# A transformer block with MLP on one core: deadline-ordered loads, DMA transposes for the first y tiles, two equal rounds of chunk widths, warming matmuls, a new item order and a new clock model

## The chip, the cores and the metric

One core of a Trainium2 chip. The time is the device time of one execution in microseconds (us). Most executions of one kernel agree within 0.3%, so this study uses five rounds a kernel, each beside runs of the kernel before on the same chip. A ratio is the mean time of one kernel's fast runs over that of the kernel before in the same rounds, so it is not quite the ratio of the medians beside it. PE is the matmul engine (TensorE) and PEld its weight loads, ACT is ScalarE, DVE is VectorE, and SPq is the queue of SyncE that issues the DMAs.

## The reference

```python
x  = A_x                                   # 2048 tokens x 1024, bf16
xn = layernorm(x)
s  = attention(xn, A_wqkv, A_wo)           # 32 heads of 32
y  = layernorm(xn)                         # a second normalisation
g  = silu(gelu(y @ B_w1 + B_b1) @ B_w2 + B_b2)   # 1024 -> 3584 -> 1024
return x + s * g
```

## The kernel before

The program is built from 512 *attention units*, four heads at a time. A unit has score matmuls on PE, two exponentials on ACT (128x1024 each), and value and sum matmuls on PE. All other matmul work is cut into *items* that fill PE between a unit's scores and the values of the unit before: `a` (first MLP matmul, one block of 128 features for one token chunk), `w` (second MLP), `q` and `v` (queries and keys, values, of the next heads), `o` (output projection). The string `PLAN` says which item goes with which unit, from unit 7 on; units 0 to 6 belong to the prologue, which normalises and transposes x. `w3` is one item cut over three units, and `.` is a unit without filler. In the views, `war` holds MLP weights, `wq` those of the projections, `hT` the first MLP's result and `gT` the second's; buffers are reused, so a name can also stand for other data.

```python
chunks = []                                # token chunks of q, a and w items
while t0 < S:                              # 352 x 5, then 288
    chunks.append((t0, min(CW, S - t0))); t0 += CW

def clock(self, x, eng, dma, c, rdy):      # estimated times, used only to order work
    ...
    elif eng == "tensor":
        mode, rounds, n = c
        one = n / 2.4 + 2.5
        span = rounds * one
        if mode != self.pe_mode:
            t = max(t, self.clk[eng] + 103.0)
            span += max(120.0 - one, 0.0)

def fill_act(u):                           # a tanh goes ahead of unit u's exponentials if it seems to fit
    ...
        if t + cost - rdy <= ATOL or u - u0 >= AGE: act_tasks.pop(0); fn()

# prologue, unit p
if p >= 2: ynorm_pro(p - 2)                # y of tiles 0 to 2 on ACT, then stored to HBM
if 4 <= p: load_sub(0, p - 4)              # first MLP weights
pair_kq(p); ...; pair_v(p)                 # 3 PSUM banks in rotation: pro_banks = [4, 5, 7]
...
if u == 5:                                 # y of the first chunk read back, transposed, from HBM
    for s4 in range(4): load_y(0, s4)
```

The clock estimate never runs on the chip. It decides, while the program is generated, in which order VectorE and ACT get their instructions. Cuts are marked with dots.

The softmax here doesn't subtract the row's maximum and nothing guards it: scores larger than these inputs give would overflow.

Of the kernel before, what the change touches and what calls it, by code (L numbers as in the profile page):

```python
# [13 lines left out]
q a v a a a . a q a v a v a a a q a a v a q a a v q a a v a a q a q a a v q a q a a a q q v a a q w3 w4 w3 w4 v w4 w2 w2 w2 a a v a q v v a q q a a a a a q a q a a q a a v a q a q q a a a v v a a a q v a a a a q q a a w3 v w3 w4 w4 w4 q v q v w2 v q w3 w3 a a a v v q a a a q a a q q a a a q q a v a q a v a a q a q a a a a v a a q a q v v v a a q q q v a q q a w3 q v q w5 q w4 w3 q w3 w4 w2 w4 a a a v v a a q a a q a q q v a a q a q v a q a a a a q a a a q a a v a a a a v a v a q a v q q w3 w4 v q w4 w4 w4 v w4 w3 w4 a a a q q a a a a v a v a a a a a v q a a v a a a q a a a v a a q q v a q q a a q a q q q a v w3 v w4 w4 q w4 w4 w4 w4 w4 a a a a q q a a q a a q a a a q a q q a a a a a a a a a a q q a a a a a q a q w2 w4 w3 w4 w2 w3 w5 o o o o o o o o o o o o w4 o o o o o o o o o o o o o o o o o o o o o o o o o o o . o o o o o o o . o o  # L14
# [21 lines left out]
class _Prog:  # L36
# [24 lines left out]
    def clock(self, x, eng, dma, c, rdy):  # L61
        t = max(self.clk[eng], rdy)
        if dma:
            self.clk[eng] = t + 60.0
            self.dma_clk = max(t, self.dma_clk) + 4.4 * c
            x.t = self.dma_clk + 1700.0
        elif eng == "tensor":
            mode, rounds, n = c
            one = n / 2.4 + 2.5
            span = rounds * one  # L70
            if mode != self.pe_mode:
                t = max(t, self.clk[eng] + 103.0)
                span += max(120.0 - one, 0.0)
            self.pe_mode = mode
            self.clk[eng] = t + span
            x.t = t + span + 140.0
        elif eng == "scalar":
            t = max(self.clk[eng], rdy + 40.0)
            self.clk[eng] = t + c
            x.t = t + c + 115.0  # L80
        elif eng == "vector":
            self.clk[eng] = t + c - 85.0
            x.t = t + c
        else:
            self.clk[eng] = t + c
            x.t = t + c
# [81 lines left out]
def bass_recurrent_scan__mha_block__mixer_channel_mlp__prompt_kernel(  # L168
# [23 lines left out]
    LAG = 1  # L192
# [7 lines left out]
    chunks = []  # L200
    t0 = 0
    while t0 < S:
        chunks.append((t0, min(CW, S - t0)))
        t0 += CW
# [6 lines left out]
    with ExitStack() as st:  # L211
# [68 lines left out]
        wq_due = []  # L280
        wq_of = {}

        def load_wq(hp, which=(0, 1, 2), lo=0, hi=DC):
            for t3 in which:
                src = A_wqkv[:, t3 * D + hp * 256:t3 * D + (hp + 1) * 256].rearrange("(c p) n -> p c n", p=128)
                op("sync", lambda e, src=src, t3=t3: e.dma_start(wq[:, t3, lo:hi, :], src[:, lo:hi, :]),  # L286
                   w=[("wq", t3, s) for s in range(lo // 2, hi // 2)], dma=f"wq{t3}{lo}", c=64 * (hi - lo))
                for s in range(lo // 2, hi // 2):
                    wq_of[t3, s] = hp

        def wq_part():
            hp, t3, lo = wq_due.pop(0)
            load_wq(hp, (t3,), lo, lo + 2)

        def wq_ready(hp, t3, dc):
            while wq_of[t3, dc // 2] != hp:
                wq_part()
# [7 lines left out]
        for tb in range(4, NT):  # L305
            load_x(tb)
        op("gpsimd", lambda e: e.iota(iota_i, pattern=[[1, 128]], base=0, channel_multiplier=-1), w=["iota"])
# [3 lines left out]

        def load_bias():
            op("sync", lambda e: e.dma_start(brow[0:FB, :], B_b1.rearrange("(fb p) -> fb p", p=128)), w=["b1r"], dma="b1", c=8)
            op("sync", lambda e: e.dma_start(brow[FB:FB + DC, :], B_b2.rearrange("(nb p) -> nb p", p=128)), w=["b2r"], dma="b2", c=8)
# [57 lines left out]
        TDMA = 4  # L372
# [6 lines left out]
        def transp(tb):  # L379
            i = tb % NXN  # L380
            if tb >= TDMA:
                op("sync", lambda e: e.dma_start_transpose(xnT[:, :, tb * 128:(tb + 1) * 128], xnb[i]),
                   r=[("xnb", i)], w=[("xnT", tb)], dma=f"xt{tb % 4}", c=256)
                return
            bk = pro_bank()

            def f(e):
                for dc in range(DC):
                    ins = e.transpose(bankb(bk)[:, dc * 128:(dc + 1) * 128], xnb[i][:, dc * 128:(dc + 1) * 128], ident[:])
                return ins  # L390
            op("tensor", f, r=[("xnb", i), "ident"], w=[("b", bk)], c=("full", 8, 128))
            op("scalar", lambda e: e.activation(xnT[:, :, tb * 128:(tb + 1) * 128],
                                                bankb(bk)[:, 0:D].rearrange("p (c t) -> p c t", c=DC), ACT.Copy),
               r=[("b", bk)], w=[("xnT", tb)], c=903.0)
# [87 lines left out]
        sp_tasks = defaultdict(list)  # L482

        def load_sub(g, q):
# [8 lines left out]
            op("sync", lambda e: e.dma_start(dst[:, lo:hi, :], src[:, lo:hi, :]), w=[("war", s, q)], dma=f"war{s}{q}", c=256)  # L493

        def load_piece(g):

            if g >= NPC:
                return
            k = g % 11
            if k < 7:  # L500
                subs = [0, 1, 2, 3]
            elif k == 7:
                subs = [0, 1, 2, 3]
            else:
                subs = [0, 1, 2, 3, 4, 5, 6]
            for i, q in enumerate(subs):
                sp_tasks[cur["u"] + i].append((load_sub, g, q))
            if k == 4:
                for i, q in enumerate((4, 5, 6)):
                    sp_tasks[cur["u"] + 1 + i].append((load_sub, g + 3, q))  # L510

        def load_y(c, s):
            t0, n = chunks[c]
            op("sync", lambda e: e.dma_start_transpose(yTc[:, 2 * s:2 * s + 2, 0:n], y_d[t0:t0 + n, 256 * s:256 * s + 256]),
               r=[("y", t) for t in toks(t0, n)], w=[("yTc", s)], dma=f"yTc{s}", c=200)

        def w1_item(c, f):
# [8 lines left out]
            def step(dc, bk):  # L526
                op("tensor", lambda e: mm4(e, lambda j: bankq(bk, j, 0, n),
                                           lambda j: w1v[s][:, dc, fo + 32 * j:fo + 32 * j + 32],
                                           yTc[:, dc, 0:n], dc == 0, dc == DC - 1),
                   r=[("war", s, dc // 2), ("yTc", dc // 2)], w=[("b", bk)], c=("col", 1, n))  # L530

            def fin(bk):
# [36 lines left out]
                if f == FB - 1 and c + 1 < NCH:  # L569
                    for s4 in range(4):  # L570
                        sp_tasks[cur["u"] + 2 + 2 * s4].append((load_y, c + 1, s4))
            return Item([lambda bk, dc=dc: step(dc, bk) for dc in range(DC)], fin, pre=pre)

        def w2_item(c, nb):
# [8 lines left out]
            def step(f, bk):  # L583
                hurry(lambda: (c, f) in have)
# [30 lines left out]
        def load_wo(h):  # L615
            op("sync", lambda e: e.dma_start(wo_sb[:, h, :], A_wo[h * 128:(h + 1) * 128, :]), w=[("wo", h)], dma=f"wo{h % 4}", c=256,
               after=[tail["xfree"]])

        def load_xres(tb):
            i4 = tb % NTB  # L620
            op("sync", lambda e: e.dma_start(xres[i4], x2[tb * 128:(tb + 1) * 128, :]), w=[("xres", i4)], dma=f"rx{i4}", c=256,
               after=[tail["xfree"]])

        def load_gres(tb):
# [5 lines left out]
               r=[("gT", nb, c) for nb in range(DC) for c in cs], w=[("gres", i4)], dma=f"rg{i4}", c=500, after=[tail["xfree"]])  # L630

        def wo_item(tb, k):
# [3 lines left out]
            def pre():  # L636
                if k == 0:
                    assert ("wo", HG - 1) in pg.lastw
                    if tb == 0:
                        for t in range(NTB):  # L640
                            load_gres(t)
                    elif tb + NTB - 1 < NT:
                        load_xres(tb + NTB - 1)
                        load_gres(tb + NTB - 1)

            def step(hc, bk):
                hurry(lambda: (hc, tb // 2) in scaled)
# [5 lines left out]
            def fin(bk):  # L653
                m = cnt["wo"]
                cnt["wo"] += 1
                f2, o3 = m % 2, tb % 3
                run_dq(pg.ready("vector", r=[("b", bk), ("gres", i4)]) + TOL)
# [68 lines left out]

        for p in range(3):
# [4 lines left out]
        def pro_unit(p):  # L732
            if p + 3 < NP:
                norm_pair(p + 3)
            if p == 3:
                load_bias()
            if p >= 2:
                ynorm_pro(p - 2)
            if 4 <= p:
# [9 lines left out]
        def ynorm_pro(tb):  # L749
            if tb < 3:  # L750
# [3 lines left out]
                op("sync", lambda e: e.dma_start(y_d[tb * 128:(tb + 1) * 128, :], xt), r=[("xst", tb)], w=[("y", tb)], dma=f"yst{tb % 4}", c=256)  # L754
# [149 lines left out]
        while u < NU + LAG or state["qi"] < total or dq or act_tasks:  # L904
# [3 lines left out]
            if u == 5:  # L908
                for s4 in range(4):
                    load_y(0, s4)  # L910
# [10 lines left out]
            if u >= NP - 1 and state["qi"] < total:  # L921
# [3 lines left out]
                for hp, which in loads.pop(qi, ()):  # L925
                    if hp < HG // 2:
                        wq_due.extend((hp, t3, lo) for t3 in reversed(which) for lo in range(0, DC, 2))
                if wq_due:
                    for _ in range(4 if qi == 0 else 1):
                        wq_part()  # L930
# [7 lines left out]
                for v in sorted(k for k in sp_tasks if k <= u):  # L938
                    for fn, *a in sp_tasks.pop(v):
                        fn(*a)  # L940
                if entry:
                    for s in it.steps[lo:hi]:
                        s(state["bank"])
                    if ys and (len(dq) < 3 or u >= 32):
                        ynorm(ys.pop(0))
                    if hi == len(it.steps):
                        it.finish(state["bank"])
                if state["qi"] == q_end:
                    tail["xfree"] = pg.lists["tensor"][-1]
                    for h in range(HG):  # L950
                        sp_tasks[u + 1 + 2 * h].append((load_wo, h))
                    for t in range(NTB):
                        sp_tasks[u + 2 + 4 * t].append((load_xres, t))
# [58 lines left out]
```

## Time and profile before

| | before |
|---|---|
| median of three runs | 1102.12 us |
| profiled span | 1098.9 us |
| PE / ACT / VectorE busy | 98% / 95% / 57% |
| unit 7 starts | 49.6 us |
| units 7 to 511 | 1031.3 us |
| after the start of unit 511 | 17.9 us |

The first lines are from the page of the kernel before: busy time of each engine, and the chain of work that ended last, by engine and by line.

```profile
...
PE 1074.6 (98%) x29089; PEld 700.4 (64%) x29089; DVE 629.1 (57%) x1413; ACT 1041.3 (95%) x1190; POOL 20.0 (2%) x63
...
q8 instruction: 228, 3.74, 1.4%
...
PE 57%; ACT 40%; DVE 1%; DMA 1%; issue 0%; SPq 0%; POOL 0%
ACT P L836 36%; PE ps L398 34%; PE ps L824 9%; PE ps L853 6%; PE ps L856 6%; ACT u L558 3%; PE ps L675 1%; PE ps L691 1%; DVE stats L326 1%; DMA OT<-in_A_x_dram 1%; ACT thz L601 0%; DMA wq<-in_A_wqkv_dram 0%; DMA xnT<-hT 0%; DVE hT L359 0%;
...
```

PE and ACT both look full and share the chain. The Trainium skill, page "Perfetto Trace Analysis", section "Identifying the Most-Contended Engine", warns that "matmul busy % (`TensorMatrix` occupancy) is not a good measure of how close you are to roofline". So I use another measure throughout. The score matmuls of each unit have their own line, and their first start in the timeline is the start of the unit. For a unit with a filler of r rounds of width n, undisturbed units of the trace fit

*floor = 0.887 us + r (n/2400 + 0.0012) us*,

that is 2.07 us for an 8-round, 352-wide item (median measured 2.073). The *excess* of a unit is its measured length less this floor, and the excess of units 7 to 511 is what PE lost: **18.5 us** before. The floor summed over all these units, 1012.8 us, is the same for both kernels. ACT needs two exponentials of 0.903 us (start to start) and about 0.68 us for each tanh, which serves two `a` items.

The timeline of PE in the prologue of the kernel before (start, duration, engine, line, operation, tile, count, and idle time ahead with what ended it):

```profile
...
7.54 1.89 PE L389 MATMUL ps<-ident,hT 128*128 128x128 bf16 x16 [7.54 <-DVE hT L359]
10.70 3.57 PE L675 MATMUL ps<-xnT,wq 128*128 128x256 bf16 x16 [1.27 <-ACT xnT L392]
...
17.44 1.92 PE L675 MATMUL ps<-xnT,wq 128*128 128x256 bf16 x16
...
21.04 0.40 PE L824 MATMUL ps<-QT,KT 32*128 32x256 bf16 x8
...
23.52 1.70 PE L675 MATMUL ps<-xnT,wq 128*128 128x256 bf16 x14 [1.53 <-DMA xnT<-hT]
```

L389 is the transposes of two tiles, L675 a query/key group, L824 the scores that begin a unit (17.11 and 21.04 us for units 0 and 1). The first group takes 3.57 us, later ones 1.92: about half the speed. At 23.52 PE waits for the DMA transpose of tiles 4 and 5.

The issuing queue (SPq) around the first filler units, and PE's waits from 49 to 66 us (total, times, longest), of the kernel before:

```profile
...
45.04 5.17 SPq L514 DMA_TRANSPOSE yTc<-y_scratch  x4
50.25 1.09 SPq L493 DMA_DIRECT2D war<-in_B_w_dram  x2
```

```profile
...
PE ps L398 <- DMA war<-in_B_w_dram: 0.7, 1, 0.7
PE ps L824 <- ACT P L836: 0.4, 1, 0.4
PE ps L824 <- issue: 0.4, 1, 0.4
PE ps L398 <- DMA wq<-in_A_wqkv_dram: 0.3, 1, 0.3
```

Four transposes of y hold the queue for 5.17 us; the first MLP's last two weight parts (`war`) are issued only from 50.25 us on, and PE waits for them.

### The profile page before, as it was taken

Reading aid. Unit: us, or ns where it says so; the run is one execution under the profiler, and the core shown is the slowest. Engines: PE = TensorE matmul, PEld = TensorE weight load, DVE = VectorE, ACT = ScalarE, POOL = GpSimd, SP = SyncE. Lnnn points to the kernel's source line nnn. Section 1 sums busy time; section 2 is a strip of 40 time slices with the busy share of each in tenths; the row PEclk is TensorE's granted clock in tenths of the full one; section 3 lists DMA queues with packets and bytes.
Section 4 is the critical chain, followed back from the end, with each engine's and each line's share of the span. In section 5 each row is a group of like instructions: output and inputs, shape, how many; then the busy total and the mean of one; then the engine's idle time right before and its main releaser. Section 6 shows DMA issues by size and latency. Waiting matters only on the chain.

```text
span 1098.9 us, 61692 instructions
## 1 busy us (share of the span) xinstructions
PE 1074.6 (98%) x29089; PEld 700.4 (64%) x29089; DVE 629.1 (57%) x1413; ACT 1041.3 (95%) x1190; POOL 20.0 (2%) x63
## 2 busy tenths in 40 slices
PE   6999999999999999999999999999999999999998
PEld 4766666666666666666666666666666666666665
DVE  8488753377742477652276852277743378624566
ACT  4799999899999999999999999999999999999994
POOL 2400000000000000000000000000000000000000
PEclk9999999999999999999999999999999999999999
DMA  8764256323373224333432334433244324386453
GB/s 249 182 204 138 77 111 175 112 80 109 95 159 96 90 80 128 99 73 105 131 121 80 118 72 133 141 112 109 80 86 136 100 93 147 112 252 115 96 143 99
DMA packets 211624, 132.97 MB, mean 121 GB/s; under 512 B 54698, under 2 KB 202154, under 8 KB 211370
## 3 DMA queue, kind: packets, MB, share of 16 engines
q1 hardware_dynamic: 211370, 129.02, 43.1%
q8 instruction: 228, 3.74, 1.4%
q14 instruction: 26, 0.21, 0.1%
HBM read 104.87 MB, written 12.58 MB: 107 GB/s over the span
## 4 chain that ended last, share of the span: by engine, by line
PE 57%; ACT 40%; DVE 1%; DMA 1%; issue 0%; SPq 0%; POOL 0%
ACT P L836 36%; PE ps L398 34%; PE ps L824 9%; PE ps L853 6%; PE ps L856 6%; ACT u L558 3%; PE ps L675 1%; PE ps L691 1%; DVE stats L326 1%; DMA OT<-in_A_x_dram 1%; ACT thz L601 0%; DMA wq<-in_A_wqkv_dram 0%; DMA xnT<-hT 0%; DVE hT L359 0%; SPq L286 0%
## 5 line engine op out<-in xcount | busy, mean ns | idle before, releaser
L836 ACT ACTIVATE P<-ps 128x1024 bf16<-128x1024 f32 x1024 | 969.7, 1075 | 16.5 <-PE ps L824 10.5
L853 PE MATMUL ps<-P,VP 128*32 128x256 bf16 x4096 | 256.6, 273 | 0.0
L856 PE MATMUL ps<-P,ones 128*32 128x256 bf16 x4096 | 256.5, 273 | 0.0
L398 PE MATMUL ps<-yTc,war 128*32 128x352 bf16 (+1 forms) x5376 | 226.2, 309 | 1.9 <-issue 1.1
L398 PE MATMUL ps<-hT,war 128*32 128x352 bf16 (+1 forms) x5376 | 225.3, 309 | 0.0
L824 PE MATMUL ps<-QT,KT 32*128 32x256 bf16 x4096 | 203.7, 273 | 8.1 <-ACT P L836 5.0
L398 PEld LDWEIGHTS ps<-yTc,war 128*32 128x32 bf16 x5376 | 127.6, 96 | 76.8 <-DVE xb L541 17.3
L398 PEld LDWEIGHTS ps<-hT,war 128*32 128x32 bf16 x5376 | 128.0, 96 | 73.9 <-issue 25.5
L597 DVE TENSOR_SCALAR zh<-ps,b2h 128x352 f32<-128x352 f32 (+1 forms) x48 | 27.5, 573 | 204.4 <-PE ps L398 204.4
L824 PEld LDWEIGHTS ps<-QT,KT 32*128 32x128 bf16 x4096 | 61.0, 92 | 120.6 <-issue 64.2
L541 DVE TENSOR_SCALAR xb<-ps,b1T 128x352 f32<-128x352 f32 (+1 forms) x168 | 96.1, 572 | 63.7 <-PE ps L398 60.0
L853 PEld LDWEIGHTS ps<-P,VP 128*32 128x32 bf16 x4096 | 109.6, 97 | 21.1 <-issue 1.5
L856 PEld LDWEIGHTS ps<-P,ones 128*32 128x32 bf16 x4096 | 109.6, 97 | 18.4
L564 DVE SCALAR_TENSOR_TENSOR hT<-u,xb 128x352 bf16<-128x352 f32 (+1 forms) x168 | 83.8, 508 | 61.3 <-ACT u L558 61.2
L398 PE MATMUL ps<-xnT,wq 128*32 128x352 bf16 (+1 forms) x2688 | 112.7, 309 | 0.0
L398 PEld LDWEIGHTS ps<-xnT,wq 128*32 128x32 bf16 x2688 | 64.0, 96 | 36.8 <-DVE xb L541 10.2
L551 DVE SCALAR_TENSOR_TENSOR u<-u,xb 128x352 f32<-128x352 f32 (+1 forms) x168 | 82.6, 508 | 1.9
L547 DVE TENSOR_TENSOR u<-xb 128x352 f32<-128x352 f32 (+1 forms) x168 | 82.6, 508 | 0.9
L558 ACT ACTIVATE u<-u 128x704 f32<-128x704 f32 (+1 forms) x84 | 70.6, 840 | 0.0
L398 PE MATMUL ps<-xnT,OT 128*32 128x352 bf16 (+1 forms) x1536 | 62.9, 309 | 0.2 <-DVE wq L658 0.2
L398 PE MATMUL ps<-wq,xnT 128*32 128x256 bf16 x1536 | 51.0, 274 | 0.3 <-DMA wq<-in_A_wqkv_dram 0.3
L398 PEld LDWEIGHTS ps<-xnT,OT 128*32 128x32 bf16 x1536 | 37.5, 97 | 19.9 <-DVE wq L658 8.1
(50 smaller groups left out, 468.1 us busy)
## 6 DMA issues: line engine op xcount, KB each, us to landing
war<-in_B_w_dram SPq DMA_DIRECT2D x336, 256.0 KB, 4.1
wq<-in_A_wqkv_dram SPq DMA_DIRECT2D x36, 128.0 KB, 4.2
OT<-in_A_x_dram SPq DMA_DIRECT2D x16, 256.0 KB, 5.6
y_scratch<-OT SPq DMA_DIRECT2D x16, 256.0 KB, 2.5
xnT<-in_A_x_dram SPq DMA_DIRECT2D x16, 256.0 KB, 4.3
out_dram<-wq SPq DMA_DIRECT2D x16, 256.0 KB, 2.0
gT_scratch<-gst SPq DMA_DIRECT2D x40, 88.0 KB, 1.7
xnT<-in_A_wo_dram SPq DMA_DIRECT2D x8, 256.0 KB, 3.6
```

What stands on the lines that cost most here:

```text
L326: op("vector", lambda e, c=c: e.bn_stats(stats[:, tb, c, :], xt[:, c * 512:(c + 1) * 512]), r=[("xst", tb)], w=[("st", tb, c)], c=677.0)
L398: ins = e.matmul(outs(j), lhsT=lhs(j), rhs=rhs, start=start, stop=stop, tile_position=(0, 32 * j), skip_group_check=True)
L541: x0 = op("vector", lambda e: e.tensor_scalar(xb[:, 0:n], bank(bk, 0, n), b1T[:, f:f + 1], None, op0=ALU.add), r=[("b", bk), "b1"], w=[kx] ...
L547: x = op("vector", lambda e: e.tensor_tensor(ub[:, 0:n], xb[:, 0:n], xb[:, 0:n], op=ALU.mult), r=[kx], w=[ku], c=151 + 1.042 * n)
L551: x = op("vector", lambda e: e.scalar_tensor_tensor(ub[:, 0:n], ub[:, 0:n], 1.0 / 0.044715, xb[:, 0:n], op0=ALU.add, op1=ALU.mult), r=[kx, ...
L558: x = op("scalar", lambda e: e.activation(ut[:, :, 0:n], ut[:, :, 0:n], ACT.Tanh, scale=0.7978845608028654 * 0.044715), r=kus, w=kus, c=48 ...
L564: op("vector", lambda e: e.scalar_tensor_tensor(hT[:, fq, 0:n], ut[:, i, 0:n], 1.0, xq[:, 0:n], op0=ALU.add, op1=ALU.mult), r=[kus[i], kq] ...
L597: x0 = op("vector", lambda e: e.tensor_scalar(zh[:, 0:n], bank(bk, 0, n), 0.25, b2h[:, nb:nb + 1], op0=ALU.mult, op1=ALU.add), r=[("b", bk ...
L824: ins = e.matmul(bank(bks[j], kh * 256, (kh + 1) * 256), lhsT=KT[i2][32 * j:32 * j + 32, k0:k0 + 128], rhs=QT[i2][32 * j:32 * j + 32, qb * ...
L836: op("scalar", lambda e, p=p, sl=sl: e.activation(pb[:, 2 * p:2 * p + 2, :, :].rearrange("p a b q -> p (a b q)"), ps[:, sl * 1024:(sl + 1) ...
L853: e.matmul(bankq(ACC, j, 0, QW), lhsT=VP[vp][:, kb, vo + 32 * j:vo + 32 * j + 32], rhs=pb[:, j, kh, :], start=first, stop=False, tile_posi ...
L856: ins = e.matmul(bankq(ACC, j, QW, 2 * QW), lhsT=ones[:, 0:32], rhs=pb[:, j, kh, :], start=False, stop=last, tile_position=(0, 32 * j), sk ...
```

## The change

Its intent: issue each load by its deadline and not before PE has come near; take y of the first chunk from SBUF by DMA transpose; have PE at full clock when x arrives; replace five chunks of 352 and one of 288 by 352, 352, 320 twice; and order all work by a clock model nearer to the chip.

```diff
 PLAN = """            # new order of the same items, 517 slots in both
-q a v a a a . a q a v a v ...
+q a a v a a a . a v a v a v ...
     def clock(...):
-            self.clk[eng] = t + 60.0
-            self.dma_clk = max(t, self.dma_clk) + 4.4 * c
+            self.clk[eng] = t + (1300.0 if c in (380, 270) else 480.0)
+            self.dma_clk = max(t, self.dma_clk) + 3.4 * c
...
-                t = max(t, self.clk[eng] + 103.0)
-                span += max(120.0 - one, 0.0)
+                t = self.clk[eng] + (98.0 if mode == "col" else 105.0)
+                t = max(t, rdy + (80.0 if mode == "row" and rdy > t else 0.0))
+                span += 11.0
-    chunks = [352, 352, 352, 352, 352, 288]      (shortened)
+    chunks = [352, 352, 320, 352, 352, 320]      (shortened)
+        def soon(prio, tag, fn, *a): ...         # loads wait in a list by deadline
+        def run_due(tag=None): ...               # issue the first, or a named one now
-    TDMA = 4                                     # tiles from 4 on transposed by DMA
+    TDMA = 6
+        def warm(e):                             # nine 512-wide matmuls on the identity
+            for i in range(9): ins = e.matmul(bank(0), lhsT=ident[:], rhs=cold, ...)
+        op("tensor", warm, r=["ident"], w=[("b", 0)], c=("full", 9, 512))
-            if p >= 2:
-                ynorm_pro(p - 2)
+            if p >= 1:
+                ynorm_pro(p - 1)
+            yturn_pro(p - 4)                     # y: DMA transpose SBUF -> SBUF
...
+                    pace[:] = pg.lists["tensor"][-1:]   # loads wait for the last matmul
+                    for _ in range(1 + (len(due) > 3)):
+                        run_due()
+                    pace.clear()
+                    soon(NPC + 16, ("gres", t), load_gres, t)  # before: at the first o item
```

## The prediction

> **What bounds the kernel.** The page of before shows PE busy 98% and ACT 95% of 1098.9 us, granted clock full. The chain of waits is 57% PE, 40% ACT, 1% DMA: neither loads nor VectorE (57%) bind on average.
>
> From the timeline I took the start of each of the 512 attention units (their score matmuls). A steady unit costs PE 0.887 us fixed (scores 0.33, values and sums 0.43, switch to filler 0.13) plus filler rounds of n/2.4 + 1.2 ns; with an 8-round, 352-wide filler the median is 2.073 us. ACT needs two exponentials of 0.903 us (start to start) and, with a first-MLP item, half a tanh of 0.68 us: 2.15 us. So runs of MLP items are ACT-bound, the rest PE-bound.
> - Unit 7, the first with filler, starts at 49.6 us.
> - Units 7 to 511 take 1031 us; the PE floor of their work is 1013: excess 18.5 us.
> - After the last exponentials: about 10 output-projection items and a store, 16 us.
>
> **What changes.** Both plans hold 517 slots with the same mix of items, 12 of them behind the last unit; the PE floor, summed over rounds, is the same. The widths move columns, not their sum. Exponentials, evictions and weight bytes stay. The change can only take idle time out; the ceiling is near 1102 - 18.5 - 3 = 1080 us.
>
> Estimates:
> 1. Prologue. The first 16 transposes take 1.89 us and the first query/key group 3.57; later ones 1.37 and 1.92. The nine warming matmuls run while PE is idle until 7.54 us. The skill page "TensorE: Matmul & The Clock Gate" (Part 1) says about 3.4 us of activity releases the half clock; the trace agrees in these durations, not in its clock row. But VectorE, whose normalised tiles 2 and 3 come at 13.6 us, swallows most of the 2 us. Tiles 4 and 5 by PE cost 1.4 us of PE and 2 us of ACT, and remove the DMA transpose that PE awaited for 1.5 us until 23.5 us. Net -1 us.
> 2. First filler units (7 to 12): the transposes of y block the issuing queue from 45.0 to 50.2 us, the last weight part goes out late, and PE waits for it and for wq: excess 3 us. Transposing y from SBUF earlier, and deadline order: -2.5.
> 3. One stall of 1.4 us at 444 us: -1, if the new order hides it.
> 4. The 288-wide chunk: PE needs 1.86 us a unit, ACT 2.1; its MLP units lose 4 us. 320 raises PE's floor to 1.96 and spreads the shortage: -2.
> 5. Other gaps (ACT just late, up to 0.5 us each, 7 us in all): a plan with a better switch cost recovers some: -2.5.
> 6. New: loads wait for a recent PE instruction, one or two a unit; a few may arrive late: +0.5.
>
> Sum about -9: 1093 us, within 2%.
>
> **What would show it.** Unit 7 starts at 48 to 49 us. No wait of PE over 0.5 us for war, wq or yTc at 50 to 60 us, none for a DMA transpose near 23 us; first query/key group about 2 us. Excess of units 7 to 511 falls from 18.5 to 8 to 12 us. Busy times of ACT and PE almost unchanged; the tail unchanged within 1 us.
>
> **What would make it wrong.** Paced loads late in the second-MLP phases (7 parts per two items) would make PE wait for war throughout: same or slower. Warm-up holding PE past 7.5 us, or added evictions delaying the prologue's exponentials, would cancel step 1. If the order fits VectorE and ACT much better, most of the 18 us goes: 1086.

## The result, and the profile after

The changed kernel takes 1100.82 us (median of 4 runs, 1099.74 to 1101.21) against 1101.55 for the kernel before in the same rounds: ratio 0.999, interval 0.9973 to 1.0008. The predicted 1093, a gain of 9 us, is missed; the change did not move the time measurably.

The page after, and PE's timeline in the prologue:

```profile
...
PE 1079.8 (98%) x29114; PEld 701.5 (64%) x29114; DVE 630.4 (57%) x1413; ACT 1043.8 (95%) x1192; POOL 20.1 (2%) x63
...
PE 54%; ACT 43%; DMA 1%; DVE 1%; SPq 0%; issue 0%; DVEq 0%
ACT P L858 39%; PE ps L394 32%; PE ps L846 9%; PE ps L875 5%; PE ps L878 5%; ACT u L564 4%; PE ps L682 1%; PE ps L698 1%; DMA xnT<-gT_scratch 0%; SPq L623 0%; ACT thz L608 0%; DMA OT<-in_A_x_dram 0%; DVE stats L322 0%; PE ps L385 0%; DVE wq
...
```

```profile
...
1.38 4.02 PE L738 MATMUL ps<-ident 128*128 128x512 bf16 x9 [1.38 <-DVE ident L309]
7.60 0.62 PE L385 MATMUL ps<-ident,hT 128*128 128x128 bf16 x8 [2.20 <-DVE hT L355]
8.41 0.74 PE L385 MATMUL ps<-ident,hT 128*128 128x128 bf16 x8 [0.19 <-DVE hT L355]
10.37 3.57 PE L682 MATMUL ps<-xnT,wq 128*128 128x256 bf16 x16 [1.21 <-ACT xnT L388]
...
21.62 1.92 PE L698 MATMUL ps<-wq,xnT 128*128 128x256 bf16 x16 [1.12 <-ACT QT L688]
23.47 0.40 PE L846 MATMUL ps<-QT,KT 32*128 32x256 bf16 x8
...
```

The warming matmuls (L738) end at 5.40 us. The transposes at 7.60 and 8.41 are faster, 0.62 and 0.74 us for 8 (before: 1.89 for 16). But the first query/key group at 10.37 us takes 3.57 us, exactly as before. At 21.62 the value group waits for the eviction of QT on ACT, a wait that the kernel before does not have. Unit 1 starts at 23.47 us where it started at 21.04, and unit 7 at 50.5 us, 0.9 us *later* than before.

The issuing queue and PE's waits after, at the first filler units:

```profile
...
42.23 1.31 SPq L773 DMA_TRANSPOSE yTc<-OT  x1
...
44.21 1.63 SPq L773 DMA_TRANSPOSE yTc<-OT  x1
...
46.51 1.94 SPq L773 DMA_TRANSPOSE yTc<-OT  x1
...
49.12 0.97 SPq L502 DMA_DIRECT2D war<-in_B_w_dram  x2
```

```profile
...
PE ps L846 <- ACT P L858: 0.4, 1, 0.4
PE ps L875 <- ACT P L858: 0.2, 1, 0.2
```

This part works: the y transposes (now from SBUF, L773) are apart, with weights between them, and PE waits for no load. Excess of units 7 to 13 fell from 3.7 to 0.6 us. Not all of these 3.1 us are the loads' doing. Unit by unit, units 8 and 9, in which PE waits for `war` and `wq`, had 1.8 us of excess before and have none after. Unit 12 lost 0.7 us before, which the view puts down to "issue" and not to a load (62.82 us; more on such stops below). And the one early unit without filler (`.`), which loses 0.64 us in both kernels, is unit 13 in the old plan and unit 14 in the new one, so its loss has only moved to the next row of the table below.

Then it is given back. Excess in us by stretch of units, each from that kernel's profile:

| units | before | after |
|---|---|---|
| 7 to 13 | 3.7 | 0.6 |
| 14 to 63 | 1.3 | 2.8 |
| 64 to 169 | 1.4 | 1.2 |
| 170 to 227 (third chunk's MLP among them) | 2.3 | 3.2 |
| 228 to 299 | 1.5 | 3.3 |
| 300 to 409 | 1.7 | 1.8 |
| 410 to 447 (sixth chunk, `a` items) | 4.0 | 1.9 |
| 448 to 469 (its `w` items, first `o`) | 2.1 | 3.1 |
| 470 to 510 | 0.6 | 0.2 |
| sum | 18.5 | 18.1 |

The spans add up: +0.85 us at unit 7, -0.36 of excess, +0.0 in the tail make +0.5 us (1098.9 to 1099.4). With the unit without filler counted on the same side, units 7 to 14 gained 2.4 us (3.7 to 1.2) and units 15 to 511 lost 2.1 (14.8 to 16.9). Questions: what happened in the prologue, and what made units 15 to 511 lose 2.1 us more?

### The profile page after: what moved, and what is told of

It reads as the page before. It is cut to its first block, busy times and chain, and to the rows that moved or that the text cites. A ratio compares the mean times of both kernels' runs of the same rounds, so it can differ in the third digit from the quotient of the medians.

```text
span 1099.4 us, 61736 instructions
## 1 busy us (share of the span) xinstructions
PE 1079.8 (98%) x29114; PEld 701.5 (64%) x29114; DVE 630.4 (57%) x1413; ACT 1043.8 (95%) x1192; POOL 20.1 (2%) x63
## 3 DMA queue, kind: packets, MB, share of 16 engines
q8 instruction: 228, 3.74, 1.4%
## 4 chain that ended last, share of the span: by engine, by line
PE 54%; ACT 43%; DMA 1%; DVE 1%; SPq 0%; issue 0%; DVEq 0%
ACT P L858 39%; PE ps L394 32%; PE ps L846 9%; PE ps L875 5%; PE ps L878 5%; ACT u L564 4%; PE ps L682 1%; PE ps L698 1%; DMA xnT<-gT_scratch 0%; SPq L623 0%; ACT thz L608 0%; DMA OT<-in_A_x_dram 0%; DVE stats L322 0%; PE ps L385 0%; DVE wq L665 0%
## 5 line engine op out<-in xcount | busy, mean ns | idle before, releaser
L858 ACT ACTIVATE P<-ps 128x1024 bf16<-128x1024 f32 x1024 | 970.3, 1077 | 16.2 <-PE ps L846 10.8
L890 DVE COPY accs<-ps 128x256 f32<-128x256 f32 x64 | 26.9, 420 | 41.9 <-PE ps L878 41.8
```

Source lines behind the costliest of these rows:

```text
L858: op("scalar", lambda e, p=p, sl=sl: e.activation(pb[:, 2 * p:2 * p + 2, :, :].rearrange("p a b q -> p (a b q)"), ps[:, sl * 1024:(sl + 1) ...
L890: op("vector", lambda e: e.tensor_copy(a[:], bank(ACC, 0, QW)), r=[("b", ACC)], w=[ka], c=425.0)
```

## The experiments

Eighteen runs (the record has none numbered e6, e8 or e10). "Unit 7" is its start and "excess" that of units 7 to 511. The last two columns split the excess; they are explained under "PE stops without a wait" below. Times are medians, in groups that share a chip and runs of the kernel before: e1 to e4; e0, e5, e7 and e9; e11 to e14; e15 to e18; e19 and e20. The second and third group ran on one and the same chip in two jobs, each other group on a chip of its own. The means of the kernel before in these two jobs are 1102.3 and 1101.8 us, so between them a ratio is the safer comparison.

| run | what it is | us | ratio to before | unit 7 | excess | stops | rest |
|---|---|---|---|---|---|---|---|
| (before) | | 1101.55 | 1 | 49.6 | 18.5 | 3.2 | 15.3 |
| (after) | | 1100.82 | 0.9990 | 50.5 | 18.1 | 1.1 | 17.0 |
| e1_nowarm | after, no warming | 1099.91 | 0.9974 | 50.6 | 16.7 | 1.6 | 15.1 |
| e2_ylate | after, y on ACT a unit later | 1099.75 | 0.9973 | 50.0 | 17.0 | 0.8 | 16.2 |
| e3_tdma4 | after, tiles 4, 5 by DMA | 1099.95 | 0.9969 | 50.0 | 17.7 | 1.1 | 16.7 |
| e4_oldpro | after, all three undone | 1099.83 | 0.9977 | 49.6 | 17.1 | 1.0 | 16.1 |
| e0_after | after again | 1101.13 | 0.9990 | 50.4 | 18.0 | 1.3 | 16.7 |
| e5_oldplan | after, old plan and widths | 1103.03 | 1.0005 | 49.6 | 21.6 | 4.8 | 16.8 |
| e7_tanh4 | after, a quarter of the tanh | 1093.27 | 0.9914 | 49.9 | 8.0 | 0.3 | 7.7 |
| e9_bridge_ylate | after, y later, long warming | 1099.68 | 0.9970 | 48.5 | 18.6 | 2.4 | 16.3 |
| e11_oldplan_neww | after, old plan | 1100.15 | 0.9982 | 50.6 | 15.4 | 0.0 | 15.4 |
| e12_newplan_oldw | after, old widths | 1103.14 | 1.0013 | 49.8 | 20.8 | 4.0 | 16.7 |
| e13_nopace | after, no pacing | 1101.07 | 0.9997 | 49.9 | 18.5 | 2.1 | 16.4 |
| e14_oldclock | after, old clock model | 1098.61 | 0.9969 | 50.0 | 16.5 | 2.8 | 13.8 |
| e15_oldplan_oldclock | after, old plan, widths, clock | 1101.84 | 0.9992 | 50.2 | 18.5 | 3.8 | 14.7 |
| e16_best | e9, old plan and clock | 1099.80 | 0.9972 | 49.0 | 17.8 | 2.1 | 15.7 |
| e17_before_neww | before, new widths | 1101.64 | 0.9990 | 49.4 | 20.5 | 5.0 | 15.5 |
| e18_best_tdma4 | e16, tiles 4, 5 by DMA | 1100.17 | 0.9978 | 50.5 | 17.5 | 2.1 | 15.3 |
| e19_sum | e9, old plan | 1098.62 | 0.9963 | 48.5 | 16.6 | 1.2 | 15.4 |
| e20_sum_gres | e19, gT transposes later | 1098.13 | 0.9956 | 48.7 | 17.1 | 2.0 | 15.1 |

Half-widths of the 95% intervals of the ratios are 0.0012 to 0.0016 (0.0018 for the first result), so two ratios of different groups that differ by less than about 0.002 are not separated. Unit 7 is not quite comparable between profiles: the first statistics start anywhere from 3.24 to 3.58 us, and the first query/key group took 3.17 to 3.57 us in profiles of the same prologue.

### The prologue: e1, e2, e3, e4

```diff
 e1: -        op("tensor", warm, r=["ident"], w=[("b", 0)], c=("full", 9, 512))
 e2: -            if p >= 1: ynorm_pro(p - 1)
     +            if p >= 2: ynorm_pro(p - 2)
 e3: -        TDMA = 6
     +        TDMA = 4
 e4: all three
```

> The changed kernel without its nine warming matmuls. Theory A (the burst ends at 5.4 us, PE is then idle for 2.2 us and half idle to 10.4 us, so the clock has fallen back and the first query/key group is cold anyway: 3.57 us with the burst): unit 7 starts within 0.3 us of 50.5 us, perhaps a little earlier, and the time stays within 1 us of the changed kernel. Rival (the burst is worth what it was written for and something else in the prologue ate it): unit 7 starts 1 us or more later, the time rises by 1 us.

Measured: unit 7 at 50.63 us, against 50.42 and 50.48 in two profiles with the burst. Theory A holds: in these profiles the nine matmuls bought nothing.

> The changed kernel with the three y normalisations on ACT one prologue unit later, as before the change had them. Theory A (the 1.25 us normalisation of tile 0 stands ahead of the evictions of query/key group 1, on which the next value group now waits, because two more transposes turned the three-bank rotation so that both use one bank): the wait of PE for the QT eviction near 21 us shrinks from 1.1 to under 0.3 us, unit 7 starts near 49.3 instead of 50.5 us, time -1 us. Rival (PE itself is the limit there, by the two extra transposes): unit 7 within 0.3 us of 50.5.

Measured: the cause is right and the size is not. Unit 1 started 5.00 us after unit 0 instead of 6.11, as the wait for the eviction went. But unit 7 came at 49.98, not 49.3. PE then met the next limit, in unit 4:

```profile
...
32.82 1.92 PE L682 MATMUL ps<-xnT,wq 128*128 128x256 bf16 x16 [1.11 <-DMA xnT<-hT]
...
```

The DMA transpose of tile 9 landed at 32.77 us, 4.6 us after its issue, where 2.8 is the median; PE lost 1.1 us.

> The changed kernel with tiles 4 and 5 again transposed by DMA. Theory A: the bank rotation is the old one, the value group no longer waits for the eviction; query/key group 2 waits for the DMA transpose until about 23.5 us again; unit 7 near 49.7 us, time -0.8 us. Rival (transposing by PE is a gain by itself): unit 7 later than 50.5 us.

Measured: unit 1 is 3.99 us after unit 0 (3.93 before the change): the rotation of banks and the two extra transposes cost PE 2.1 us there. Unit 7 at 49.99: about 0.5 us gained, less than the 0.8 expected, since the wait for the DMA transpose returns.

> All three prologue pieces undone (no warming matmuls, tiles 4 and 5 by DMA, y normalisations as before), y of the first chunk still transposed from SBUF. Theory A: unit 7 back at 49.6 us with the first filler units still free of stalls (excess of units 7 to 13 at 0.6 instead of 3.7 us); time about -0.9 us against the changed kernel. Rival: the start up stall of the kernel before comes back with the old prologue.

Measured: unit 7 at 49.58, where it was before, and units 7 to 13 have an excess of 1.2 us instead of 3.7. So the gain of the first filler units does not need the new prologue. In time the four are alike (means 1099.6 to 1100.4, standard errors 0.3 to 0.6); only the profiles separate them.

### The changed kernel again, and a warming without a hole: e0, e9

> The changed kernel itself, so that it shares a chip and its runs of the kernel before with the next three. Ratio 0.997 to 1.000 as on record, excess of units 7 to 511 near 18 us, unit 7 at 50.5 us.

Measured: ratio 0.9990, unit 7 at 50.42, excess 18.0. It repeats.

```diff
 e9: e2, and
-            for i in range(9):                  # in warm
+        transp(0); one warming matmul; transp(1); five warming matmuls
+            18 warming matmuls ahead of transp(0) instead of 9
```

> The changed kernel with y normalised one unit later and with the warming drawn out: 18 matmuls before the first transposes, 1 between the two, 5 after them, so that PE has no idle stretch before the first query/key group. Theory A (the burst failed because the clock fell back in the idle stretch): the first query/key group takes about 1.9 us instead of 3.57, and unit 1 starts 2 to 3 us sooner than 23.5 us. But the normalised tiles and their DMA transposes arrive at a cadence of their own, so unit 7 gains less: 49 to 50 us instead of 50.5, time -1 us. Rival (the first group is slow for another reason, such as late weights): it stays at 3.5 us.

Measured, in PE's timeline of e9:

```profile
...
1.37 7.00 PE L738 MATMUL ps<-ident 128*128 128x512 bf16 x18 [1.37 <-DVE ident L309]
...
10.94 1.91 PE L682 MATMUL ps<-xnT,wq 128*128 128x256 bf16 x16 [0.38 <-ACT xnT L388]
...
21.18 0.40 PE L848 MATMUL ps<-QT,KT 32*128 32x256 bf16 x8
...
```

The same query/key group takes 1.91 us instead of 3.57, and unit 7 starts at 48.46 us, 2.0 us sooner than in e0. Of that, e2's later y alone had given 0.5. The time is 1.5 us less (1099.68 against 1101.13 on the same chip). The granted clock shows why. This is the line for 10 to 16 us of the windows view (busy time of PE, weight loads, VectorE, ACT and POOL, then the granted clock, the DMA share and GB/s), first of the changed kernel, then of e9:

```profile
...
10.00:16.00 6.00, 5.63 (x37) 4.61 (x38) 5.04 (x12) 2.05 (x5) 2.59 (x7) 0.53 1.04 374
...
```

```profile
...
10.00:16.00 6.00, 5.58 (x60) 4.09 (x59) 5.01 (x13) 3.64 (x6) 2.59 (x7) 1.00 1.07 395
...
```

0.53 against 1.00. The clock records of the changed kernel give full clock from 5.35 to 8.76 us, half from 8.76 to 15.59, then full to the end. The Trainium skill, page "TensorE: Matmul & The Clock Gate", Part 1, says that the clock needs about 3.4 us of activity and falls back after an idle window of the same length, and that the window is free-running. The records agree with the length: 3.41 and 6.83 us. In the window from 5.35 to 8.76 PE had the last 0.05 us of the burst and about one us of transposes, and it ended at half clock. So the prediction read the page for the warming and not for the falling back. The other profiles show that the burst was not even sure to warm PE: in five of the eleven with these nine matmuls (e2, e5, e7, e12, e14) no full clock is recorded before 13.2 us, and the first 8 transposes took 1.03 us, as without a burst.

### What the gaps after the start up are: e7

```diff
-  e.activation(ut[:, :, 0:n], ut[:, :, 0:n], ACT.Tanh, ...)
+  e.activation(ut[:, :, 0:n // 4], ut[:, :, 0:n // 4], ACT.Tanh, ...)   # wrong result on purpose
```

> The changed kernel with the first MLP's tanh on a quarter of its columns (a wrong result on purpose): ACT has about 0.45 us less in each of 84 pairs, nothing else changes. Theory C (the gaps after the start up are PE waiting for ACT to free score banks, not loads): the excess of units 14 to 511 falls from 17.5 to under 8 us, time about -10 us. Rival (loads, or VectorE freeing filler banks): excess falls by less than 3 us.

Measured: the result is wrong (relative error 0.027), the time 1093.27 us, 7.9 us less than e0, and the excess of units 14 to 511 fell from 17.4 to 7.0 us. The chain of waits of e7 is nearly all PE, where the changed kernel had 43% ACT:

```profile
...
PE 90%; DVE 4%; ACT 3%; DMA 2%; SPq 0%; issue 0%; POOL 0%; DVEq 0%
...
```

So most of the excess is PE waiting for ACT, not for loads. (The profile is of the fastest of e7's five runs, 1090.49 us, so its excess flatters e7 a little.)

### Plan, widths, pacing, clock model: e5, e11, e12, e13, e14

```diff
 e5:  old PLAN and old widths in the changed kernel     e11: old PLAN only    e12: old widths only
 e13: -                    pace[:] = pg.lists["tensor"][-1:]
      +                    pace[:] = []
 e14: the three edits of clock() undone
```

> The changed kernel (loads, prologue, clock model) with the old plan and the old widths. Theory B (the plan and widths gave back after the start up what the start up gained: units 14 to 511 were 14.8 us over the floor of PE before and are 17.5 now): the start up excess stays at 0.6 us, the rest falls to about 15 us, total 15 to 16, time 2 us less than the changed kernel. Rival (what came back comes from the loader's pacing or from the order on VectorE under the new clock model): the rest stays at 17 to 18 us with the old plan too and the time does not move.

Measured: theory B, that plan and widths were what gave the gain back, falls. With both undone the kernel is slower (1103.03 against 1101.13) and its excess 21.6 us. (Units 7 to 13 have 1.5 us here and not 0.6, since the unit without filler is unit 13 again.)

> The changed kernel with the old plan, keeping the new widths. The old plan with the old widths (e5) had 21.6 us of excess, the new with the new 18.0. If the widths do it: the last MLP items (units 410 to 447) fall from 4.7 us of excess to about 2 and the third chunk (units 170 to 227) rises by about 1, time between e5 and the changed kernel, about 1 us less than e5's. If the plan's order does it: same as e5.

Measured: faster than either (means 1099.8 against 1101.2 for e0 and 1102.9 for e5). The widths gain 3.1 us under the old plan (2.5 by the ratios, since the jobs differ). Beside the new widths, the *new plan* loses 1.4 us by the means, but only 0.9 by the ratios, which their intervals do not separate. In the profiles most of it stands in units 448 to 469 (3.3 us of excess in e0, 1.2 in e11): the new plan puts its first `o` item before the last `w` items, and in e0 unit 461 waits there for a gT transpose (shown at the end of the next section). In units 410 to 447 the excess fell from e5's 4.7 to 1.9 us, and in units 170 to 227 it rose from 1.7 to 3.1, as expected.

> The changed kernel with the old widths under the new plan. If the widths only move the shortage of ACT from the sixth chunk to the third and sixth: units 410 to 447 rise to about 4 us of excess, units 170 to 227 fall to about 2, total within 1 us of the changed kernel's 18. If the widths are a gain: 2 us more.

Measured: mean 1103.1, 1.9 us slower than e0; units 410 to 447 at 4.4 us, units 170 to 227 at 1.4. Here too the widths gain.

> The changed kernel without the wait of loads for a recent matmul (the loads keep their order and the waits that their buffers need). If pacing costs or gains nothing on the critical path: time and excess within 1 us of the changed kernel, loads land as before it. If paced loads come late: excess 2 us less. If pacing keeps loads out of the way of urgent ones: excess rises, the first filler units (7 to 13) above all.

Measured: 1101.07 us, the same as the changed kernel. Pacing is neither the loss nor a gain.

> The changed kernel with the old clock model, which only decides the order of work on VectorE and ACT. If the new model is what costs after the start up (tanh set among the exponentials at worse places): units 14 to 447 fall from 14 us of excess to 11 or less, time -3 us. If it helps as meant: excess rises by 1 us or more. If it does not matter: within 1 us.

Measured: 1098.61 us, mean 2.9 us less than e0 (2.3 by the ratios). Units 14 to 447 fell only from 13.9 to 12.7 us of excess, not to 11. Both programs have the same order of instructions on PE and in the load queue; only ACT and VectorE are ordered otherwise, ACT in some twenty places. One place, the timelines of e0 (first) and of e14 in unit 289, a value item of only 256 columns, whose floor is 1.75 us. e0, on PE and on ACT:

```profile
...
630.34 0.40 PE L846 MATMUL ps<-QT,KT 32*128 32x256 bf16 x8
...
630.67 1.06 PE L394 MATMUL ps<-wq,xnT 128*32 128x256 bf16 x32
630.74 0.89 ACT L564 ACTIVATE u<-u 128x704 f32<-128x704 f32 x1
...
632.60 0.40 PE L846 MATMUL ps<-QT,KT 32*128 32x256 bf16 x8 [0.44 <-ACT P L858]
...
```

and e14:

```profile
...
629.16 0.40 PE L845 MATMUL ps<-QT,KT 32*128 32x256 bf16 x8
...
629.48 1.06 PE L393 MATMUL ps<-wq,xnT 128*32 128x256 bf16 x32
...
630.91 0.40 PE L845 MATMUL ps<-QT,KT 32*128 32x256 bf16 x8
...
633.24 0.88 ACT L563 ACTIVATE u<-u 128x704 f32<-128x704 f32 x1
```

In e0 the tanh (`u<-u`, 0.89 us) stands ahead of the exponentials of this short unit, and the next scores wait: the unit takes 2.26 us. In e14 the same kind of unit takes 1.75 us, and the tanh comes two units later. My reading, which no run tests: the new model sees a longer switch of PE, so it believes that ACT has room for a tanh where it has none. And this is only part of what e14 gained. In e14 other value units lose as much (units 18, 30, 194 and 349: 0.3 to 0.5 us each); without the stops explained below, the 48 value units together lose 4.4 us in e0 and 3.7 in e14. The largest single difference is no tanh. It is unit 461, which loses 1.3 us in e0 and nothing in e14, and there PE waits for VectorE, which waits for a gT transpose. This is e0's line of PE's waits from 900 to 1000 us; e14 has none like it:

```profile
...
PE ps L394 <- DVE wq L665: 1.3, 1, 1.3
...
```

So e14 shows that the new model costs time. Of the tanh as its cause it shows about 0.6 us; 1.3 us is this one wait, and the rest is spread.

### Settling the account: e15, e17

> The new loads and prologue alone: old plan, old widths, old clock model. Excess of units 7 to 511 was 18.5 us before, and 21.6 with the new loads, prologue and clock model (e5). If the new clock model cost those 3 us and the 3 us of the start up: total 16 to 17, time 4 us less than e5's 1103. If the new loads cost them (late gT for the first output items above all, units 448 to 469): total stays at 20 to 21, with over 4 us in units 448 to 469.

Measured: neither. Excess 18.5, time 0.9992. The ratio is 1.3 parts in 1000 below e5's, which points the way of e14, though the two intervals do not separate them. But units 448 to 469 keep 4.8 us, as the rival had it. What it is came from the next look.

**PE stops without a wait.** In e15, PE's timeline holds stops in the middle of a run of equal matmuls:

```profile
...
979.02 1.65 PE L393 MATMUL ps<-hT,war 128*32 128x288 bf16 x47
981.45 0.54 PE L393 MATMUL ps<-hT,war 128*32 128x288 bf16 x9 [0.77 <-issue]
...
984.79 1.16 PE L393 MATMUL ps<-hT,war 128*32 128x288 bf16 x31
986.84 0.42 PE L393 MATMUL ps<-hT,war 128*32 128x288 bf16 x5 [0.89 <-issue]
...
```

I first took them for late weights, because two DMA transposes of gT hold the queue for 1.8 us each just ahead of the last weight loads. But the stops come after 47 and 31 matmuls, where no new weight part begins (parts have 16 matmuls of four rounds), and the view names no releaser ("issue"). The packet records of the instruction queue give another reading. They show 228 packets of 16 KB, at the median one every 4.6 us: one for each 255 of PE's 58,178 matmuls and weight loads. In the kernel before, one packet begins at 436.26 us and the next only at 443.56; it ends at 444.49, and PE resumes at 445.95 us after a stop of 1.1 us (the "1.4 us stall" of the prediction). In e15 packets end at 980.07 and 985.29, and PE resumes at 981.45 and 986.84. In the 20 profiles here I counted 73 places after 66 us where two matmuls of one tile stand over 0.3 us apart; 66 of them end 1.1 to 1.8 us after such a packet ended, a range that chance would hit about one time in seven. That is a correlation, not an experiment: late instruction packets fit it, but no run here delays or removes them. The column "stops" in the table sums places of this kind (each less 0.1 us): from unit 7 on, over 0.25 us, and ending 1.1 to 1.8 us after a packet; e16's is without a true wait of that length, told below. They sum to 3.2 to 4.8 us in the four profiles with the old widths and to 0 to 2.8 us in those with the new ones, save e17's 5.0. But for the two kernels with the old loads the sum takes in the wait for `war` in unit 8, which is no stop of this kind by the view: counted after 66 us only, the kernel before has 1.7, e12 3.6 and e17 3.2, and the two kinds of widths are not clearly apart.

With the stops taken out, the "rest" reads more plainly: 16.4 to 17.0 in every profile with the new plan and the new clock model whose prologue is unchanged; 13.8 with the old clock model (e14); 15.1 to 15.4 with the old plan, the new widths and the new clock model (e11, e19, e20). Where only the prologue differs (e1 to e4, e9) it is 15.1 to 16.7: another prologue shifts the clock estimates and with them the order.

> The kernel before with nothing changed but the widths. If the widths are a gain of their own (the 288-wide chunk's MLP units lost 4 us to ACT; 320 in two chunks): excess falls from 18.5 to 14 to 16 us, time -3 us, ratio 0.997. If they only help beside the new loads: within 1 us of the kernel before.

Measured: 0.9990, excess *up* to 20.5 us; both of my expectations on the gain fall; what came is the other branch, within 1 us of the kernel before. The profile shows one reason, a wait at unit 448 that the new widths meet with the old plan and the old clock model, here (shown) and in e16 and e18 (1.4 and 1.5 us):

```profile
...
PE ps L394 <- DVE hT L560: 1.5, 1, 1.5
...
```

The first `w` item of the last chunk comes before VectorE has finished the last `hT` block: 1.9 us of excess in all three. With the new clock model it is not there (0.1 us in e11), which is one reason why e16 did not add up.

### Putting the parts together: e16, e18, e19, e20

```diff
 e16: e9 with the old PLAN and the old clock model       e18: e16 with TDMA = 4
 e19: e9 with the old PLAN
 e20: e19, and the first four gT transposes are issued in the first o item, as before the change
```

> New widths and new loads, old plan, old clock model, y normalised one unit later, warming drawn out to the first query/key group. If the parts add up (unit 7 at 48.5 us as in e9, excess 14 us: 15.4 as in e11 less about 1 for the clock model): 1096 us, ratio 0.994 to 0.995, faster than every kernel so far. If they do not add up: 0.997 or more.

Measured: 0.9972. They do not add up, for the wait at unit 448 and 2.1 us of stops.

> e16 with tiles 4 and 5 by DMA again. If transposing them by PE pays once PE stays warm and y is out of the way: 0.5 to 1 us slower than e16, unit 7 about 49. If it costs (1.4 us of PE, 2 us of ACT): faster than e16 by as much.

Measured: 0.9978, the same in time within the intervals; unit 7 at 50.5 instead of 49.0, since PE waited for a DMA transpose:

```profile
...
PE ps L681 <- DMA xnT<-hT: 2.1, 1, 2.1
...
```

So with PE warm and y out of the way, the transposes of tiles 4 and 5 by PE pay in the profile, by 1.5 us. Part of that is again the clock: after the wait it is recorded at half from 22.66 to 26.07 us, and the query/key group at 22.70 takes 3.55 us instead of 1.91.

> e11 (new loads, new clock model, new widths, old plan) with the drawn out warming and the later y of e9. If these parts add up: unit 7 near 48.5 to 49 us (e9: 48.46), excess of units 7 to 511 near 15.5 to 16.5 us (e11: 15.4, without e16's wait of 1.9 us at unit 448), time 1097 to 1098, ratio 0.995 to 0.996. If not: 0.997 or more.

Measured: 0.9963 (1098.62 against 1103.44), unit 7 at 48.5, excess 16.6. They add up nearly: time, ratio and excess each lie a little above what was expected, and below the "if not".

> e19 with the first four gT transposes issued at the first output item, as before, instead of with the other loads of the tail. In e15 two of them held the issuing queue for 1.8 us each just ahead of the last second-MLP weights, and PE waited 0.8 and 0.9 us for those. If that is what units 448 to 469 lose under the new loads: their excess stays at or under 2 us and PE has no wait over 0.4 us there; time 0 to 1 us less than e19. If not: units 460 to 463 keep waits of 0.5 to 1.2 us.

Measured: 0.9956, interval 0.9942 to 0.9969: the lowest ratio of all correct kernels, 4.9 us (0.44%) under the kernel before by the ratio. Against e19 it is 0.5 us, not separable. Units 448 to 469 lost 1.7 us and not 2.1, but one stop of 0.5 us stayed, and by then the theory that the gT transposes delay the weights had lost its main witness in e15. What remains of it is the changed kernel itself, at its first `o` item, which the new plan places before the last `w` items:

```profile
...
979.13 1.29 SPq L636 DMA_TRANSPOSE xnT<-gT_scratch  x1
979.53 0.53 DVE L665 TENSOR_TENSOR wq<-ps,xnT 128x352 f32<-128x352 f32 x1 [1.32 <-DMA xnT<-gT_scratch]
...
980.11 1.14 PE L394 MATMUL ps<-hT,war 128*32 128x320 bf16 x28 [0.93 <-DVE wq L665]
...
```

There VectorE waits 1.3 us for a gT transpose and PE 0.9 us for VectorE.

## Why the prediction was wrong, point by point

The prediction summed six terms to about -9 us (as listed they make -8.5). The profiled span moved by +0.5, the medians by -0.7. Two steps failed: that PE, once warmed, stays warm (term 1), and that an order made with a truer clock model is a better order (term 5). The start up's term (2) came nearly as forecast, and the other two gave back what it gained.

1. **"Prologue ... Net -1 us": wrong sign, +0.85 us at unit 7.** The step that failed is the first sentence on the warming: I took it that PE, once warm at 5.4 us, would be warm at 10.4. The clock had fallen back at 8.76 us (0.53 granted from 10 to 16 us), and the group took 3.57 us again. Two smaller omissions: the y normalisation of tile 0, 1.25 us on ACT, was moved ahead of the QT eviction, and two more transposes turned the bank rotation so that the value group waits for that eviction (1.1 us; e2). "VectorE swallows most of it" was too dark: at unit 7, e9 stands 1.5 us ahead of e2, from which it differs only by the longer warming.
2. **"First filler units: -2.5": right in kind, somewhat large.** The loads gave 1.8 us (units 8 and 9; e4 keeps it with the old prologue). The excess of units 7 to 14 fell by 2.4, with 0.7 from the stop in unit 12, which the new loads are not shown to have removed.
3. **"One stall of 1.4 us at 444 us: -1": not a property of the order.** Such stops move between profiles of one program (unit 457 lost 1.3 us in one profile of the changed kernel, 0.2 in the next) and fit late instruction packets: this one ended 1.46 us after a packet, that of unit 457 1.59 us after one (there the view names ACT as what ended it, so it is less sure).
4. **"The 288-wide chunk: -2": right direction.** Units 410 to 447 gained 2.1 us, the third chunk's stretch lost some of it, and by the mean times the widths are worth 1.9 us (e12 against e0) and 3.1 us (e5 against e11), 2.5 in both by the ratios. Much of that stands in the profiles as fewer stops (4.0 and 4.8 us with old widths, 1.3 and 0.0 with new), so it is not mainly the reason that I gave. And alone (e17) they gained nothing measurable.
5. **"A plan with a better switch cost recovers some: -2.5": the step that failed most.** It has the other sign. The new clock model costs 2.3 to 2.9 us (e14): tanh in short units is about 0.6 us of that, a wait of 1.3 us for a gT transpose in unit 461 is the largest single part. The new plan costs 0.9 to 1.4 us beside the new widths (e11), which is not clear of noise. I took an order made with a truer model of PE for a better order, with nothing from the trace to show it.
6. **"Loads wait ...: +0.5": nothing (e13).**

So where did the gain go? The start up gained 2.4 us (units 7 to 14), of which 1.8 are shown to be the loads. 0.85 us was lost ahead of it and 2.1 us after it. In the profile of the changed kernel two units, 457 and 461, hold 2.3 us (0.1 before): 461 waits for a gT transpose, and 457 lost only 0.2 us with the same program in e0. Everything else after unit 14 cancels: 3.5 us more in units 15 to 63 and 170 to 299, as much less in the others, 2.1 of it in units 410 to 447. The mechanism of the bound was right: the floor did not move, idle time was all there was to win, and e7 shows that most of it belongs to ACT. That the later loss is ACT's too is not shown: the waits for ACT that the view lists from 69 to 1083 us sum to 4.0 us before and to 4.7 after, 1.1 of these in unit 457.

Open: what delays the instruction packets, and why the widths seem to bear on it; whether the changed kernel with the old clock model *and* e9's prologue would beat e20 (e14's gain and e9's gain were measured apart, never together); which single moved tanh costs what, of which I showed one; and whether `o` items kept behind the last `w` items would free the new order of its wait in unit 461.

## What to carry to other kernels

A warm clock must be kept up to the work that needs it: fill the hole, not only the start. A truer cost model need not give a better order, so test it alone before it is trusted. When two engines are both near full, short work of the second that lands in a unit in which the first has little to do can cost time there: read the unit, not the average. And when stretches are compared, check that the same items lie in them: here one unit without filler moved 0.64 us across a boundary.

## What the Trainium skill lacked or had wrong

- "TensorE: Matmul & The Clock Gate", Part 1: right, and the part on falling back is the one that counts here. A burst of 4.02 us that ended at 5.40 us did not keep a group at 10.37 us warm (3.57 us against 1.91 in e9); before 15.59 us full clock was recorded from 5.35 to 8.76 us only. In five of eleven profiles a burst of the same length released nothing. A recipe for bridging would help: 18 matmuls ahead, one and five between the transposes were enough.
- "Trainium Architecture — The Big Picture", section "The software stack", says that instruction streams are copied to the engines when the program is loaded. The traces show 228 packets of 16 KB (3.74 MB) in an instruction queue all through the run. That is on another page, "Runtime: NRT & Kernel Launch", section "Instruction fetch mechanics", which has refills in blocks of 16 KiB and calls their cost mostly hidden. The stops of PE here, up to about 1.6 us and ending 1.1 to 1.8 us after a packet, would be a cost that is not hidden, if the packets cause them, which no run shows.
- No page that I found gives how long a DMA transpose of this size holds the issuing queue on this chip. Here it was 1.2 to 2.3 us for nearly all (1.26 at the median), against about 0.3 to 0.6 us for most plain loads. Those of xn in e2 landed 2.8 us after issue at the median, tile 9 after 4.6 us.
